# Retention and gated FFN on one core: scaled k through the crossbar, half of the masks moved from VectorE to ScalarE and GpSimd

## Chip, core and metric

The kernel runs on one core of one Trainium2 chip. The metric is the device time of one launch in microseconds (us). The engines are TensorE (PE, with its weight loads as PEld), VectorE (DVE), ScalarE (ACT), GpSimd (POOL) and SyncE (SP, which here only issues DMAs).

## The reference

Two stages follow each other. The first is a retention layer over 4 batches, 8 heads, 768 tokens and 64 features per head, with one decay per head:

```
gamma[h] = 1 - 2**(-5 - h);  scale = 1/8
state = gamma * state + outer(k[t], v[t])        # per batch and head, 64 x 64
y[t]  = scale * q[t] @ state
```

The heads of one token are then joined to a row x of 512, and a gated FFN follows: `(sigmoid(x @ w_gate) * (x @ w_val)) @ w_out`, with widths 512, 1536, 512, over 3072 rows. Inputs and output are float32; the matmuls run in bfloat16.

## The kernel before

**Tiling.** The 768 tokens are cut into 6 chunks of 128 (a chunk index is a tile t of the FFN: 4 batches x 128 tokens = 512 rows). A chunk has two pairs P of batches, so there are 12 pairs, P = 2t and 2t + 1; a pair has two batches c = 0, 1. Heads lie two by two on the 128 partitions: i = 0 the even heads, i = 1 the odd ones, p = 0 to 3 the four twos.

**Retention in a chunk.** `scores` (sc) multiplies k and q of a batch, transposed in qkT, into two PSUM banks, one for even and one for odd heads. `mask` (mk, L243) multiplies a bank by a table that holds the decay and the triangle, and writes st in bfloat16; it runs on DVE. `inter` (in) multiplies the state of the past (zbd) with q, `intra` (ia) adds v times st, `y_out` (yo) scales the sum by the row decay taby0 and writes xT, the FFN's input. `scaled` (kt, L228 and L231) makes kt, k times a decay of its token; `state` (sm) multiplies kt and v, `state_sum` (zs) adds it to the running state on DVE, `state_out` (zo, L295) copies it to zbd on ACT. The last two pairs need no kt.

**Transposing.** Pairs 0 to 3 are transposed on PE (tp, te); pairs 4 to 11 by the crossbar, a transposing DMA that SP issues (xk for k, xq for q, L219). It reads kn, the loaded k.

**Loads** are issued by POOL (L96). Pairs 6 to 11 come in three groups lk6, lq6, lv6, lk8, ..., lk10, ..., each for two pairs. Ahead of lk stands ho (`hold`, L561), a small POOL copy that reads the last element of the crossbar's output, so that the next k isn't loaded before the crossbar has read the last one.

**FFN.** From the second tile on, products of 2 x 2 blocks take 7 multiplications instead of 8: gp (gate) and vp (value) are single products into shared PSUM banks, where gc and vc (ACT copies, L430 and L409) take an intermediate value out of a bank before a later product adds onto it: product 3 of a block adds onto the bank that copy 5 has read, products 4, 6 and 7 onto the one that copy 1 has read. ga and va add on DVE, gs is the sigmoid on ACT, vf and vd multiply on POOL and DVE. dp, dc, da and ds do the same for the output projection; ds is the store. The sums that these need of weights and activations are aw, dw, wp, hg (POOL), ad, dd, xs, hs (DVE) and wc (ACT). Tile 0 and half of tile 1 use plain or half projections (gm, vm, ag, av, bg, bv) with sg, as, bs on ACT and mu, am, bm on DVE.

**Order.** Nothing is left to a scheduler. `ORDER` is a list of such steps written out, six strings, one for each tile's time; the number behind a name picks the block, + or - shift the tile by one. A step in capitals issues whole matmuls (128 columns of weights, L305), in small letters two halves of 64 columns (L309). Each engine executes its instructions in this order and waits at the first one that isn't ready. `PLACES` gives the buffer of each new tile by hand; PSUM has 7 banks for all but the state.

Of the kernel before, what the change touches and what calls it, by code (L numbers as in the profile page):

```python
# [9 lines left out]
F32 = mybir.dt.float32  # L10
# [7 lines left out]
def kernel(  # L18
# [14 lines left out]
    C = 128  # L33
# [22 lines left out]
        "ob": "01231012302130102302132031",  # L56
        "gs": "01234501234503215034203502345102354130524301453201540321453034035412031524",
        "maskd": "01",
        "ff": (
            "012345601230465102346523105426310524631205312063451623541063254165413240653016035062153621063526"  # L60
            "301263063210232534013260652605123601624302143545634210420422603216325041254246536024012416250305"
            "340153041501230163420254135426032013541354162053132620412051534"
        ),
        "qkT": "010231230123",
        "kt": "0101100101",
        "st": "012345670123456702134675120346752104637563245710",
        "xT": "010101",
        "hT": "010101",
        "scr": "010101101001101010010101010101",
# [62 lines left out]
    tok = const.tile([128, 2], F32, name="tok")  # L132
    nc.gpsimd.iota(tok, pattern=[[C, 2]], base=-C, channel_multiplier=1, allow_small_or_imprecise_dtypes=True)
# [11 lines left out]
    nc.vector.memset(lsc, math.log(scale))  # L145
    lgp = const.tile([128, NP], F32, name="lgp")
# [15 lines left out]
    tabk = const.tile([128, 2, H], F32, name="tabk")  # L162
# [13 lines left out]
    def tile_mask(i):  # L176
        nc.gpsimd.affine_select(maskd[:, i], tabk[:, 1, i:H:2].unsqueeze(2).to_broadcast([128, NP, C]),
                                pattern=[[0, NP], [1, C]], base=0, channel_multiplier=-1,
                                compare_op=ALU.is_ge, fill=0.0)

# [35 lines left out]
    def xbar(P, i):  # L216
        if P not in qkT:
            new_qkT(P)
        nc.sync.dma_start_transpose(out=qkT[P][:, i].rearrange("d c p s -> d (c p) s"),  # L219
                                    in_=(kn, qn)[i][P].rearrange("s g d -> s (g d)"))  # L220

    def scaled(P, h):
# [4 lines left out]
        if P < 4:  # L227
            nc.vector.tensor_tensor(to, x, tabk[:, 0, :].unsqueeze(1).unsqueeze(3).to_broadcast([C, 2, H, D]),  # L228
                                    op=ALU.mult)
        else:  # L230
            nc.scalar.activation(to[:, :, h, :], x[:, :, h, :], AX.Copy, scale=tabk[:, 0, h:h + 1])  # L231
# [9 lines left out]
    def mask(P, c, i):  # L241
        st[P, c, i] = place(at, [128, NP, C], BF16, tag="st", name="st")
        nc.vector.tensor_tensor(st[P, c, i], sc[P, c][i], (mask0 if P < 2 else maskd)[:, i], op=ALU.mult)  # L243
# [356 lines left out]
    y_step(1, 0, "av")  # L600
    y_step(1, 1, "av")
# [16 lines left out]
    for s in range(4):  # L618
# [61 lines left out]
        "mk": lambda t, n: mask(n // 4, n // 2 % 2, n % 2),  # L680
        "yo": lambda t, n: y_out(n // 2, n % 2),
# [115 lines left out]
```

## Time and profile before

| | |
|---|---|
| time, median of 3 runs | 217.46 us (217.25 to 217.79) |
| time of the profiled execution | 217.96 us |
| its span | 216.2 us |
| PE clock granted, mean | 0.992 |
| instructions | 7308 |
| HBM read, written | 28.31 MB, 6.29 MB |

The span runs from the first to the last instruction of the profiled execution. An engine's busy time counts its instructions' own spans; matmuls are pipelined, so that a busy PE needn't be PE at its peak. A row of a group reads: line, engine, operation, output <- inputs (partitions x elements and type), count | busy us, mean ns of one | idle us ahead of them and what ended it. A row of the chain or the timeline begins with its start and its length in us.

### The profile page before, as it was taken

What the parts mean: (1) busy time and instruction counts of PE and PEld (TensorE: products, weight loads), DVE (VectorE), ACT (ScalarE), POOL (GpSimd) and SP (SyncE); (2) the same over time, 40 slices, a digit from 0 to 9 for tenths busy, and PEclk for the clock granted to TensorE, in tenths of its full rate; (3) what the DMA queues carried; (4) which work ended last, traced back from release to release, by engine and by line L of the source; (5) the groups of instructions that cost most, each with busy time, mean ns of one, the idle gap of its engine ahead of it and who ended that gap; (6) DMA issues with size and microseconds to landing.
All of it is one profiled execution on the core that took longest, in us unless ns stands there. A gap on an engine that the chain in (4) does not pass through costs nothing.

```text
span 216.2 us, 7308 instructions
## 1 busy us (share of the span) xinstructions
PE 205.0 (95%) x3002; PEld 178.3 (82%) x3002; DVE 188.1 (87%) x406; ACT 147.8 (68%) x397; POOL 139.7 (65%) x145
## 2 busy tenths in 40 slices
PE   6678999999999999999999999989999999999993
PEld 6465555888888998898988889988999988888883
DVE  5677879899899999979999899978899999968961
ACT  6384365534993489887779798866768979577621
POOL 8976784879899946699564299756528537025400
PEclk9889999999999999999999999999999999999999
DMA  9999999999991999999992059996022000003504
GB/s 127 141 171 194 197 172 162 188 195 158 155 127 24 119 160 200 211 63 160 159 245 66 0 36 183 127 215 134 3 93 104 3 3 0 3 3 84 115 34 162
DMA packets 103922, 25.38 MB, mean 117 GB/s; under 512 B 93904, under 2 KB 101072, under 8 KB 103888
## 3 DMA queue, kind: packets, MB, share of 16 engines
q0 software_dynamic: 81104, 13.90, 83.6%
q1 hardware_dynamic: 22640, 10.88, 27.0%
q8 instruction: 23, 0.38, 0.7%
q14 instruction: 11, 0.09, 0.2%
q10 hardware_dynamic: 144, 0.13, 0.2%
HBM read 28.31 MB, written 6.29 MB: 160 GB/s over the span
## 4 chain that ended last, share of the span: by engine, by line
PE 87%; DVE 8%; issue 1%; ACT 1%; ACTq 0%; DVEq 0%
PE ff L309 39%; PE ff L305 37%; PE ff L238 3%; PE ff L258 2%; PE ff L536 2%; DVE scr L414 2%; PE ff L200 2%; PE z L280 1%; DVE hT L332 1%; DVE gs L435 1%; DVE qkT L210 1%; DVE ws L361 1%; DVE xT L273 1%; DVE kt L228 1%; ACT xT L271 1%
## 5 line engine op out<-in xcount | busy, mean ns | idle before, releaser
L420 POOL TENSOR_TENSOR hT<-gs,scr 128x512 bf16<-128x512 f32 x17 | 22.1, 1300 | 22.4 <-DVE scr L414 9.9
L430 ACT COPY gs<-ff 128x256 f32<-128x256 f32 x72 | 25.6, 377 | 11.6 <-PE ff L309 7.1
L414 DVE TENSOR_TENSOR scr<-scr,ff 128x512 f32<-128x512 f32 (+1 forms) x48 | 25.7, 550 | 4.8 <-ACT scr L409 1.5
L409 ACT COPY scr<-ff 128x256 f32<-128x256 f32 x72 | 25.2, 375 | 6.6 <-PE ff L309 3.3
L435 DVE TENSOR_TENSOR gs<-gs,ff 128x512 f32<-128x512 f32 (+1 forms) x48 | 25.8, 550 | 3.2 <-PE ff L305 2.0
L510 ACT COPY ob<-ff 128x256 f32<-128x256 f32 x48 | 17.8, 375 | 15.7 <-PE ff L305 9.2
L440 ACT ACTIVATE gs<-gs 128x512 f32<-128x512 f32 (+1 forms) x48 | 24.8, 530 | 2.8 <-DVE gs L435 2.7
L243 DVE TENSOR_TENSOR st<-ff,maskd 128x512 bf16<-128x512 f32 x40 | 25.8, 686 | 0.5 <-PE ff L238 0.4
L309 PE MATMUL ff<-xT,wg 128*64 128x256 bf16 (+1 forms) x268 | 24.0, 308 | 0.1
L309 PEld LDWEIGHTS <-wg 128*64 128x64 bf16 x356 | 19.7, 110 | 3.8 <-issue 0.2
L423 POOL TENSOR_TENSOR hT<-gs,scr 128x256 bf16<-128x256 f32 x16 | 11.9, 744 | 16.2 <-ACT gs L440 12.4
L309 PE MATMUL ff<-xT,wv 128*64 128x256 bf16 (+1 forms) x224 | 21.9, 311 | 0.0
L309 PEld LDWEIGHTS <-wv 128*64 128x64 bf16 x324 | 18.0, 110 | 4.1 <-issue 0.3
L309 PE MATMUL ff<-xs,ws 128*64 128x256 bf16 x228 | 20.5, 273 | 0.6 <-issue 0.6
L309 PEld LDWEIGHTS <-ws 128*64 128x64 bf16 x340 | 18.9, 110 | 1.4 <-issue 1.3
L305 PEld LDWEIGHTS <-wv 128*128 128x128 bf16 x178 | 17.2, 98 | 2.3
L305 PEld LDWEIGHTS <-hT 128*128 128x128 bf16 x174 | 16.8, 98 | 2.7 <-issue 0.6
L305 PEld LDWEIGHTS <-wg 128*128 128x128 bf16 x162 | 15.7, 98 | 4.1 <-issue 2.1
L231 ACT ACTIVATE kt<-kn,tabk 128x128 bf16<-128x128 bf16 x48 | 18.4, 407 | 0.1
L305 PE MATMUL ff<-xT,wv 128*128 128x256 bf16 (+1 forms) x132 | 18.1, 276 | 0.0
L305 PE MATMUL ff<-wo,hT 128*128 128x256 bf16 x132 | 17.7, 272 | 0.2 <-DVE ob L515 0.2
L305 PE MATMUL ff<-xT,wg 128*128 128x256 bf16 x110 | 15.6, 272 | 1.6 <-ACT xT L271 0.9
(119 smaller groups left out, 529.8 us busy)
## 6 DMA issues: line engine op xcount, KB each, us to landing
out_dram<-ob SPq DMA_DIRECT2D x18, 256.0 KB, 4.8
vn<-in_v_dram POOLq DMA_DIRECT2D x6, 256.0 KB, 11.9
wo<-in_moe_w_out_dram POOLq DMA_DIRECT2D x4, 384.0 KB, 13.2
kn<-in_k_dram POOLq DMA_DIRECT2D x3, 512.0 KB, 7.7
qn<-in_q_dram POOLq DMA_DIRECT2D x3, 512.0 KB, 10.0
vn<-in_v_dram POOLq DMA_DIRECT2D x3, 512.0 KB, 11.6
out_dram<-ob SPq DMA_DIRECT2D x11, 128.0 KB, 2.3
kn<-in_k_dram POOLq DMA_DIRECT2D x5, 256.0 KB, 12.1
```

The costliest lines, as they stand in the source:

```text
L231: nc.scalar.activation(to[:, :, h, :], x[:, :, h, :], AX.Copy, scale=tabk[:, 0, h:h + 1])
L243: nc.vector.tensor_tensor(st[P, c, i], sc[P, c][i], (mask0 if P < 2 else maskd)[:, i], op=ALU.mult)
L305: nc.tensor.matmul(o, left, right, skip_group_check=True, **kw)
L309: nc.tensor.matmul(o[half], left[:, half], right, skip_group_check=True, **kw)
L409: nc.scalar.copy(vals[t, g][:, {1: 0, 5: 2, 3: 1}[n]], m[False][:, 256:] if n == 1 else m[True][:, :256])
L414: nc.vector.tensor_tensor(o, o, x, op=ALU.add)
L420: eng.tensor_tensor(h[:, 2 * g], s, vals[t, g][:, 0:2].rearrange("p two n -> p (two n)"), op=ALU.mult)
L423: eng.tensor_tensor(h[:, 2 * g + 1, 256:], s[:, 256:], vals[t, g][:, 2], op=ALU.mult)
L430: nc.scalar.copy(o, pairs[t, g, 0][x][:, :256] if x else pairs[t, g, 0][x][:, 256:])
L435: nc.vector.tensor_tensor(o, o, pairs[t, g, 0][False][:, cols], op=ALU.add)
L440: nc.scalar.activation(o, x, AX.Sigmoid)
L510: nc.scalar.copy(o, fast[t, i][x][:, :256] if x else fast[t, i][x][:, 256:])
```

## The change

The decays are rearranged so that one scaling of k serves both the scores and the state. The token table loses its offset: kt is now k times gamma^(-s) with s the place in the chunk, and the row decay taby0 has gamma^(C + t) instead of gamma^t (C = 128).

For pairs 4 to 9 the crossbar reads kt instead of kn. Their scores then carry the token's decay already, and what is left of the mask is a constant per head, gamma^(-C), and the triangle. The even heads' masks of these pairs stay DVE multiplications, with a new table maskc, built by one POOL select (mt0). The odd heads' masks (12 of them) are split into two steps: mc, four ACT copies of 128 columns from PSUM with the constant as scale, and ms, one POOL select in place that cuts the triangle. The crossbar of these pairs now waits for the eight scalings of its pair.

The scaling of pairs 2 and 3 goes from one DVE instruction to eight on ACT. The outputs of pair 1's two batches are written by DVE and ACT, one each, where before both engines wrote half of each. ORDER and PLACES are new throughout; among much else 9 of the hs sums go to POOL (hg), 5 of the POOL sums aw to DVE (ad), and 4 of the products vf to DVE (vd).

```diff
-    tok = const.tile([128, 2], F32, name="tok")
-    nc.gpsimd.iota(tok, pattern=[[C, 2]], base=-C, channel_multiplier=1, allow_small_or_imprecise_dtypes=True)
+    tok = const.tile([128, 3], F32, name="tok")
+    nc.gpsimd.iota(tok[:, :2], pattern=[[C, 2]], base=0, channel_multiplier=1, allow_small_or_imprecise_dtypes=True)
...
+    nc.vector.memset(tok[:, 2:], float(C))
...
+    def chunk_mask(i):
+        if not maskc:
+            maskc[0] = place(at, [128, 2, NP, C], F32, tag="maskd", name="maskc")
+        nc.gpsimd.affine_select(maskc[0][:, i], tabk[:, 2, i:H:2].unsqueeze(2).to_broadcast([128, NP, C]),
+                                pattern=[[0, NP], [1, C]], base=0, channel_multiplier=-1,
+                                compare_op=ALU.is_ge, fill=0.0)
...
-                                    in_=(kn, qn)[i][P].rearrange("s g d -> s (g d)"))
+                                    in_=(qn if i else kt if P < NPAIR - 2 else kn)[P].rearrange("s g d -> s (g d)"))
...
-        if P < 4:
+        if P < 2:
             nc.vector.tensor_tensor(to, x, tabk[:, 0, :].unsqueeze(1).unsqueeze(3).to_broadcast([C, 2, H, D]),
...
-        nc.vector.tensor_tensor(st[P, c, i], sc[P, c][i], (mask0 if P < 2 else maskd)[:, i], op=ALU.mult)
+        nc.vector.tensor_tensor(st[P, c, i], sc[P, c][i], (mask0 if P < 2 else maskd if P < XBAR or P > NPAIR - 3 else maskc[0])[:, i],
+                                op=ALU.mult)
+
+    def mask_copy(P, c, i):
+        st[P, c, i] = place(at, [128, NP, C], BF16, tag="st", name="st")
+        for p in range(NP):
+            nc.scalar.activation(st[P, c, i][:, p], sc[P, c][i][:, p], AX.Copy, scale=math.exp(-C * lg[2 * p + i]))
+
+    def mask_cut(P, c, i):
+        nc.gpsimd.affine_select(st[P, c, i], st[P, c, i], pattern=[[0, NP], [1, C]], base=0, channel_multiplier=-1,
+                                compare_op=ALU.is_ge, fill=0.0)
...
-    y_step(1, 0, "av")
-    y_step(1, 1, "av")
+    y_step(1, 0, "v")
+    y_step(1, 1, "a")
```

The parts of the new order of which the prediction speaks, first from the scores of pairs 4 and 5 to tile 1's products, then around lk8:

```diff
+ ... sm5 sc9 mk18 sc8 mk16 dw22 zs5 mc19 mc17 ms17 BG8 DP03- wc5 DP16- dd17 ms19 zo4 BV4 IN8 dd2 sc11 in9 ia9
+ bs8 ho5 in10 ia8 sm4 mc23 lk6 sc10 mc21 DP02- bm4 DP01- dc01- wp11 mk22 IN11 zo11 dc03- wc4 yo9 BV8 da16-
+ mk20 kt49+ kt52+ ad2 yo8 dw18 zs4 kt53+ kt59+ bm8 GP21+ gp22+ ms23 gc21+ kt57+ ad6 kt61+ ia11 kt58+ yo11
+ dp06-- da06-- av8- ms21- ia10- yo10- zo10- xs0 dp17-- da17-- dp07-- gp05 gc05 gp25 gc25 kt48 DP14-- dc14--
+ ds14-- GP15 am8- kt50 hs4- xs2 da07-- GP23 ...
+ ... VP15 kt62 sm7 VP07 xk6- ... xq6- ... xk7- ... ds16-- ... GP36 xq7- ... vf16 ho7 ... sc12 ... sc15 mc31 lk8
+ ... gp55 lq8 lv8 gc55 ia12 kt71 VP51 vc51 GP46 GP53 gc53 zs7 kt65 mk26 GP51 da16- DP17- vc41 gc51 ... GP56 ...
```

More of the change, by code (lines that the diff above doesn't have):

```diff
@@ L55 @@
         "v": "010101",
-        "ob": "01231012302130102302132031",
-        "gs": "01234501234503215034203502345102354130524301453201540321453034035412031524",
-        "maskd": "01",
+        "ob": "01231030321023032103121032",
+        "gs": "01234501235435012453205431501423051402530104521325402153201421401235042135",
+        "maskd": "010",
         "ff": (
-            "012345601230465102346523105426310524631205312063451623541063254165413240653016035062153621063526"
-            "301263063210232534013260652605123601624302143545634210420422603216325041254246536024012416250305"
-            "340153041501230163420254135426032013541354162053132620412051534"
-        ),
-        "qkT": "010231230123",
-        "kt": "0101100101",
-        "st": "012345670123456702134675120346752104637563245710",
+            "012345601230465102346523105426314021635160412036412041362413062541520145634163041203621042310423"
+            "142324064216524131305416521504250423623164120210524163131321205234123465254054315614316216345040"
+            "534605364632304210651613402605240512631261204356462412032122543"
+        ),
+        "qkT": "012301230123",
+        "kt": "0120102010",
+        "st": "012345670123456703216745021345670265741326507413",
         "xT": "010101",
         "hT": "010101",
-        "scr": "010101101001101010010101010101",
+        "scr": "010110011001101010100110010101",
     }
@@ L161 @@
         nc.vector.memset(z, 0.0)
-    tabk = const.tile([128, 2, H], F32, name="tabk")
+    tabk = const.tile([128, 3, H], F32, name="tabk")
     tabz = const.tile([128, NP], F32, name="tabz")
@@ L177, in tile_mask @@
         nc.gpsimd.affine_select(maskd[:, i], tabk[:, 1, i:H:2].unsqueeze(2).to_broadcast([128, NP, C]),
+                                pattern=[[0, NP], [1, C]], base=0, channel_multiplier=-1,
+                                compare_op=ALU.is_ge, fill=0.0)
+    maskc = {}
+    def chunk_mask(i):
+        if not maskc:
+            maskc[0] = place(at, [128, 2, NP, C], F32, tag="maskd", name="maskc")
+        nc.gpsimd.affine_select(maskc[0][:, i], tabk[:, 2, i:H:2].unsqueeze(2).to_broadcast([128, NP, C]),
                                 pattern=[[0, NP], [1, C]], base=0, channel_multiplier=-1,
@@ L680 @@
         "mk": lambda t, n: mask(n // 4, n // 2 % 2, n % 2),
+        "mc": lambda t, n: mask_copy(n // 4, n // 2 % 2, n % 2),
+        "ms": lambda t, n: mask_cut(n // 4, n // 2 % 2, n % 2),
+        "mt": lambda t, n: chunk_mask(n),
         "yo": lambda t, n: y_out(n // 2, n % 2),
```

148 rows, old and new, of the table ORDER are left out of this document.

## The prediction, made before the changed kernel was run

> **What bounds the kernel now.** I read the page's engine totals and its chain of waits first, then the stretches (busy time by window), then the chain in order of time.
>
> ```profile
> PE 205.0 (95%) x3002; PEld 178.3 (82%) x3002; DVE 188.1 (87%) x406; ACT 147.8 (68%) x397; POOL 139.7 (65%) x145
> ```
> ```profile
> PE 87%; DVE 8%; issue 1%; ACT 1%; ACTq 0%; DVEq 0%
> ```
> ```profile
> 0.00:18.70 18.70, 12.61 (x156) 10.64 (x156) 11.85 (x32) 11.96 (x32) 15.22 (x23) 0.91 1.70 152
> 32.00:36.00 4.00, 3.67 (x58) 2.28 (x56) 3.93 (x10) 3.59 (x5) 2.88 (x4) 1.00 2.16 167
> 108.00:112.00 4.00, 3.85 (x77) 3.38 (x72) 3.90 (x9) 2.67 (x8) 3.25 (x3) 1.00 1.42 211
> 140.00:152.00 12.00, 11.02 (x206) 10.39 (x204) 9.84 (x27) 8.26 (x25) 7.64 (x8) 1.00 1.05 159
> 176.00:204.00 28.00, 27.94 (x256) 24.74 (x254) 24.72 (x56) 20.83 (x63) 11.15 (x11) 1.00 0.14 32
> 204.00:212.90 8.90, 8.56 (x76) 7.10 (x74) 5.55 (x14) 2.49 (x7) 0.00 (x0) 1.00 0.31 98
> ```
> ```profile
> 64.35 0.55 PE ff L238 x16
> 69.63 0.37 PE z L280 x16
> 132.16 0.22 PE ff L258 x8
> 140.54 0.64 issue
> 147.85 0.34 issue
> 176.70 24.47 PE ff L305 x222
> ```
>
> The first number of a stretch after its length is PE's busy time. PE is idle for 6.1 us before 18.7 us, where the operands first arrive. From there to 212.9 us its idle time is 0.33 + 0.15 + 0.98 + 0.06 + 0.34 = 1.9 us in these five stretches, and none in the others. Of that, 0.98 us (140 to 152 us) is "issue", which no engine ended; 0.9 us is the most that a relieved VectorE (DVE) can give back. PE is granted its full clock (1.00) after the start, and 222 matmuls of 256 columns take 24.47 us, 0.110 us each. The steps of the order hold the same count of matmuls after the change as before (168 gate products, 168 value products, 84 down products, 24 half projections, 22 whole ones, the same scores; some only change between the form of two halves and the whole form). So PE's own work doesn't move: the change can win 0.9 us in the middle and something at the two ends, and it loses every wait that the new order brings to PE.
>
> **The change, part by part.** Engine work first, from the groups of instructions by line and shape.
>
> ```profile
> L243 DVE TENSOR_TENSOR st<-ff,maskd 128x512 bf16<-128x512 f32 x40 | 25.8, 686 | 0.5 <-PE ff L238 0.4
> L228 DVE TENSOR_TENSOR kt<-kn,tabk 128x1024 bf16<-128x1024 bf16 x4 | 4.9, 1218 | 0.0
> L231 ACT ACTIVATE kt<-kn,tabk 128x128 bf16<-128x128 bf16 x48 | 18.4, 407 | 0.1
> L177 POOL TENSOR_SCALAR_AFFINE_SELECT maskd<-tabk 128x512 f32<-128x512 f32 x2 | 1.2, 644 | 0.0
> L295 ACT CAST zbd<-za 64x512 bf16<-64x512 f32 x20 | 12.4, 618 | 4.5 <-DVE za L287 2.6 <-DVE za L290 0.9 <-PE ff L305 0.8
> ```
> ```profile
> 77.32 0.62 ACT L430 COPY gs<-ff 128x256 f32<-128x256 f32 x2
> 110.89 0.69 ACT L231 ACTIVATE kt<-kn,tabk 128x128 bf16<-128x128 bf16 x2
> ```
>
> DVE loses 12 masks (25.8/40 = 0.65 us each, 7.7 us) and two scalings of k (1.22 us each, 2.4 us): 10.1 us of 188. ScalarE (ACT) gains 16 scalings (18.4/48 = 0.38 us each, 6.1 us) and 48 copies of 128 columns. The trace has no such copy. Two copies of 256 columns take 0.62 us, so the second adds 0.25; half of it, 0.13, is the low end. Two scalings of 128 columns take 0.69, so the second adds 0.30: the high end. I take 0.20, between them, because the copy has the shape of the one and the fixed scale of the other. One mask's four copies are then 0.8 us (0.5 to 1.2), and ACT has 148 + 6 + 10 = 164 us of 216. GpSimd (POOL) gains 13 selects, priced at the 0.64 us of L177, 8.4 us. Neither engine is full on average, so what matters is who waits for whom.
>
> ```profile
> L474 DVE TENSOR_TENSOR hs<-hT,hs x13: 411/424/1379, 56.5 to 206.7; 128x512 bf16<-128x512 bf16 x13
> L474 DVE TENSOR_TENSOR hs<-hs,hT x12: 414/420/1375, 28.2 to 204.6; 128x512 bf16<-128x512 bf16 x12
> ```
>
> The DVE gain is worth at most the 0.9 us above. Against it, some DVE sums with two SBUF operands already take 1.38 us where the median is 0.42, and the selects put more POOL reads beside them; I take 0.7 us of gain (0 to 0.9). The Trainium skill ("SBUF — State Buffer", section "Who interferes with whom") says that a VectorE instruction with two SBUF inputs and a GpSimd instruction that reads SBUF exclude each other, and the second blocks fully. By that rule, which the 1.38 us agree with, the select could cost DVE what its masks saved, and the 0.7 would be 0.
>
> **Scaling ahead of the crossbar.** A scaling now stands between k's load and k's crossbar, and the order puts scalings into ACT's queue soon after the load's issue. An engine works in order, so everything behind such a scaling waits for the load.
>
> ```profile
> kn<-in_k_dram POOLq DMA_DIRECT2D x3, 512.0 KB, 7.7
> vn<-in_v_dram POOLq DMA_DIRECT2D x3, 512.0 KB, 11.6
> qkT<-kn SPq DMA_TRANSPOSE x8, 8.0
> qkT<-qn SPq DMA_TRANSPOSE x8, 6.0
> ```
> ```profile
> 68.62 0.18 POOL L561 COPY kept<-qkT 128x2 bf16<-128x2 bf16 x1
> 68.75 1.72 POOL L96 DMA_DIRECT2D kn<-in_k_dram  x1
> ```
> ```profile
> 77.01 0.40 ACT L231 ACTIVATE kt<-kn,tabk 128x128 bf16<-128x128 bf16 x1
> ```
>
> Before, the load of pairs 6 and 7 (lk6) was issued at 68.75 us, landed 7.7 us later (76.5), and the first scaling that needs it ran at 77.0: nothing waited. After, POOL must make two masks (ms17, ms19) before ho5 and lk6, and they wait for ACT's copies, which wait for the scores. Counted from the start of step sc8: two copy steps 1.6 + 0.1, two selects 1.3, ho5 0.15, so lk6 goes out at 3.15 and lands at 10.85. ACT comes to kt49 at 8.4: PE is through IN11 at 6.9, and zo11, dc03 and wc4 follow (1.5). There it waits; behind kt49 lie kt52, kt53, kt59 (with kt49 4 x 0.30 = 1.2), gc21 (0.27), kt57, kt61, kt58 (0.9), zo10 (0.62), gc05 (0.27), gc25 (0.38): gc25 is done at 14.5. PE's step GP23 adds onto the bank that gc25 reads and can't start before. PE's work from sc8 to GP23, by the new order: 3 scores at 0.28, 4 half projections at 8 x 0.11 = 0.88, 8 down products at 0.66, 8 inter or intra steps at 0.22, one state step 0.37, 5 products at 0.22: 0.84 + 3.52 + 5.28 + 1.76 + 0.37 + 1.10 = 12.9. PE waits **1.6 us**. With 0.5 or 1.2 us for a mask's copies it is 1.0 or 2.4.
>
> The Trainium skill ("DMA: Bandwidth & Descriptors", section "Anatomy of one DMA — SWDGE (gpsimd) path") fits such a load as 2.0 us plus its bytes over 436 GB/s, an estimate of 3.2 us for 512 KB. By that k would land at 6.4, before ACT comes to it, and the wait would be 0; the row of 7.7 us disagrees, and the row decides.
>
> The same again for pairs 8 and 9: xq7 (6.0 us to land) releases ho7 and lk8 (7.7 us), and the order puts kt71 close behind. From xq7's place in the order, 0.2 + 6.0 + 7.7 = 13.9, then kt71, vc51, gc53, kt65, vc41, gc51 (1.8 us) before PE's GP56: 15.7, where PE has 13.1 us of work between (GP36 at its place to GP56, summed in the same way). That is 2.6 us if SP issues xq7 at its place; SP may run ahead by up to the 3.5 us since VP15 (kt62, the last scaling that xk7 needs, follows it), and then it is nothing. I take **0.9** (0 to 2.6). The first crossbars of pairs 4 and 5 have room: their scores come some 10 us after the scalings. The load of v for pair 7 (lv6) stands behind a POOL sum that waits for DVE (hg5 for hs4), about 9 us before sm7 uses it: nothing at the 7.7 us of k, 2.4 us at the 11.6 of v, where other loads were in flight; I take 0, and the 2.4 goes to the range.
>
> **Both ends.**
>
> ```profile
> L148 DVE MEMSET lgp<- 64x1 f32 x8 | 0.5, 59 | 0.3
> ```
> ```profile
> 16.72 0.38 ACT xT L268
> 17.12 0.77 DVE xT L269 x2
> 17.93 0.81 PE ff L305 x6
> ```
> ```profile
> 212.36 0.38 ACT ob L510
> 212.76 0.37 ACTq L531
> 213.23 0.37 ACT ob L510
> ```
>
> The start gains one memset ahead of the identity (about 0.1 us) and splits pair 1's output by half instead of within each half: DVE waited until 17.12 for ACT and PE until 17.93; one instruction on each engine should save 0.15 us or, if the two writes to one tile are put in sequence, cost 0.3. I take 0 for the start (-0.3 to 0.4). At the end the order puts dc04 ahead of dc14, so ACT's store issue (0.37 us and its gaps) no longer stands before the last copy: **-0.4** (-0.5 to 0).
>
> Sum on the profiled execution (217.96 us, 1.8 us over its span of 216.2): 217.96 + 1.6 + 0.9 - 0.7 - 0.4 = 219.4. The median of the runs is 217.46, 0.5 below that execution, so I forecast **218.9 us**.
>
> **Rivals.** (1) Faster: ACT's holds are hidden, because k lands sooner (less traffic beside it) or PE arrives later at GP23 and GP56 for other reasons. Both waits go, and the time is 217.46 - 0.7 - 0.4 = 216.4; with the start's best, 216.0, and if the "issue" idle went too, 215.1. It decides at about 6 us for lk6: from there the hold is hidden. For it: PE has waits that I don't foresee, which shorten these. Against it: all three k loads of this size have a median of 7.7. Chance 0.29.
> (2) No change: one wait is half hidden, the gains cancel the rest: 217.46 - 1.1 + 1.2 = 217.6. Chance 0.13.
> (3) Worse: the copies take 0.30 us each, v is late for sm7 and xq7 leaves at its place: 217.46 + 2.4 + 2.4 + 2.6 - 1.1 = 223.8; with two of the three 221.4. ACT, then, is the bound between 70 and 110 us. Chance 0.13.
> (4) The relief doesn't come, since the selects hold DVE: 219.6, within my forecast's case, which has 0.45 with it.
>
> The measurement tells about 0.3% (0.65 us) from no change. Slower is the forecast's case and (3), 0.58; within 0.3% is (2), 0.13; faster is (1), 0.29. The range leaves out the best of (1) and the worst of (3): 215.4 to 222.0.
>
> **What would show it.** In the changed profile: ACT idle before L231 with a DMA of kn as what ended it, some 3 us near 74 us and again near 104; PE idle 1 to 2 us near 80 us, ended by ACT's copy; POOL's masks of 0.64 us; DVE near 178 us busy; the last copy not behind a store issue. Wrong it is if ACT shows no such wait, if lk6 lands in under 6 us, or if PE's idle time between 18.7 us and the end is under 1.9 us.

## The result, and the profile after

The changed kernel takes 224.44 us (median of 4 runs, 222.85 to 232.78), the kernel before 217.62 us beside it (217.25 to 217.79). The ratio is 1.029, with a 95% interval of 1.023 to 1.035. The forecast was 218.9 us, in a range of 215.4 to 222.0: slower was right, the size was not. The ratios here and below leave out executions more than 1.5% above the fastest of their kernel.

The profiled execution of the changed kernel is the longest of its four (232.78 us), so I also read the profile of a second, unaltered submission, called the repeat here (223.82 us, span 222.0). First the busy times and the chain of the changed kernel's page, then of the repeat's:

```profile
PE 208.8 (90%) x3050; PEld 178.8 (77%) x3050; DVE 189.4 (82%) x392; ACT 158.2 (68%) x460; POOL 151.5 (66%) x158
PE 64%; DVE 14%; DMA 7%; POOL 5%; ACT 4%; issue 4%; DVEq 0%; POOLq 0%; ACTq 0%
```
```profile
PE 206.3 (93%) x3050; PEld 177.5 (80%) x3050; DVE 185.7 (84%) x392; ACT 158.4 (71%) x460; POOL 151.3 (68%) x158
PE 71%; DVE 21%; ACT 4%; issue 2%; POOL 1%; DVEq 0%; POOLq 0%
```

PE's share of the chain fell from 87% to 64 and 71%; DVE, DMA and POOL stand there in its place. And DVE, with 189.4 and 185.7 us, is about as busy as before (188.1), although it lost some 10 us of work. The stretches of 44 to 84 us, first of the repeat and then of the kernel before, say where (after the length come the busy times of PE, PEld, DVE, ACT and POOL):

```profile
44.00:62.00 18.00, 14.98 (x256) 13.99 (x256) 16.27 (x26) 11.01 (x29) 14.49 (x14) 1.00 1.94 160
62.00:84.00 22.00, 21.14 (x333) 18.38 (x330) 20.61 (x43) 16.94 (x53) 17.36 (x21) 1.00 0.88 73
```
```profile
44.00:62.00 18.00, 18.00 (x219) 15.71 (x217) 16.93 (x31) 12.05 (x28) 16.46 (x16) 1.00 1.96 166
62.00:84.00 22.00, 22.00 (x383) 20.20 (x381) 21.47 (x46) 14.28 (x39) 18.07 (x19) 1.00 1.50 114
```

PE loses 3.0 us between 44 and 62 us, a place of which the prediction has no term, and 0.9 us between 62 and 84, the place of its first wait. In the timeline, the repeat's PE waits there twice, for a mask and for a product of DVE; the changed kernel's first profile has one wait of 9.1 us:

```profile
48.93 1.03 PE L326 MATMUL ff<-xT,wv 128*128 128x256 bf16 x8 [1.45 <-DVE st L254]
58.74 1.06 PE L330 MATMUL ff<-xT,wv 128*64 128x256 bf16 x16 [1.58 <-DVE hT L370]
```
```profile
57.85 1.86 PE L326 MATMUL ff<-xT,wv 128*128 128x256 bf16 x8 [9.08 <-DVE st L254]
```

In the first profile eight matmuls took 1.86 us after that wait, in the repeat 1.03. The page's row of the granted clock, in slices of 5.8 us, says why:

```profile
PEclk9999999995599999999999999999999999999998
```

It is 0.5 for two slices, 52 to 63.6 us, that is from within the wait to some 5 us behind it; at half the clock those 5 us held some 2 us less work (an estimate). What held DVE stands in its own timeline and in POOL's, in the repeat:

```profile
45.91 2.37 DVE L495 TENSOR_TENSOR hs<-hT,hs 128x512 bf16<-128x512 bf16 x1
48.20 1.28 DVE L254 TENSOR_TENSOR st<-ff,maskd 128x512 bf16<-128x512 f32 x2
53.79 0.28 DVE L382 TENSOR_TENSOR ws<-wv 128x256 bf16<-128x256 bf16 x1
53.99 4.10 DVE L382 TENSOR_TENSOR ws<-wg,ws 128x256 bf16<-128x256 bf16 x1
58.01 0.68 DVE L370 TENSOR_TENSOR hT<-gs,ff 128x512 bf16<-128x512 f32 x1
```
```profile
45.66 1.14 POOL L96 DMA_DIRECT2D vn<-in_v_dram  x1 [0.58 <-DMA wo<-in_moe_w_out_dram]
46.82 1.17 POOL L477 TENSOR_TENSOR scr<-wo 128x512 f32<-128x512 bf16 x1
47.94 0.83 POOL L187 TENSOR_SCALAR_AFFINE_SELECT maskc<-tabk 128x512 f32<-128x512 f32 x1
48.74 1.15 POOL L477 TENSOR_TENSOR scr<-scr,wo 128x512 f32<-128x512 f32 x1
...
55.67 1.15 POOL L477 TENSOR_TENSOR wt<-wo,scr 128x512 bf16<-128x512 bf16 x1
56.79 1.14 POOL L477 TENSOR_TENSOR scr<-wo 128x512 f32<-128x512 bf16 x1
60.80 1.16 POOL L477 TENSOR_TENSOR scr<-scr,wo 128x512 f32<-128x512 f32 x1 [2.87 <-ACT wt L481]
```

From 46.82 us, right behind the issue of a load, to 57.9 us POOL runs ten sums and a select without a pause, seven of them the weight sums wp of L477, each reading two SBUF operands. A DVE sum with two SBUF operands that takes 0.29 us alone took 4.10 us and ended at 58.09, just behind POOL's row. The sum at 45.91 (0.42 us alone) began during the issue of the load and ended at 48.28, behind the first weight sum. The issue can hold such a sum too: in the kernel before one of 0.29 us took 0.72 at 29.72, beside nothing else. The masks of L254, with one operand in PSUM, ran beside the same POOL sums in 0.64 us each.

The first profile has four long sums in a row there, of 2.05, 2.97, 2.86 and 3.11 us, each ending shortly behind the end of a POOL instruction, but the last three not behind the first that ended: the one below passed the ends at 48.88 and 49.99 and ended at 51.28, behind the third, at 51.10.

```profile
48.31 2.97 DVE L382 TENSOR_TENSOR ws<-wv 128x256 bf16<-128x256 bf16 x1
```

The kernel before has the same weight sums, and most of DVE's instructions beside them have a PSUM operand. But nine DVE sums with two SBUF operands run there too, between 46.9 and 66 us, and none took over 1.38 us: the seven that were held each ended shortly behind the POOL instruction that was running. Three of them, and POOL's instruction beside the last two:

```profile
51.20 1.24 DVE L361 TENSOR_TENSOR ws<-wv,ws 128x256 bf16<-128x256 bf16 x1
56.51 1.38 DVE L474 TENSOR_TENSOR hs<-hT,hs 128x512 bf16<-128x512 bf16 x1
60.99 1.24 DVE L361 TENSOR_TENSOR ws<-ws,wg 128x256 bf16<-128x256 bf16 x1
```
```profile
56.27 1.34 POOL L456 TENSOR_TENSOR wt<-wo,scr 128x512 bf16<-128x512 bf16 x1
60.75 1.34 POOL L474 TENSOR_TENSOR hT<-hT 128x512 bf16<-128x512 bf16 x1
```

So the new order doesn't bring more such sums beside POOL's. What differs in this stretch is that DVE got its turn at the end of one POOL instruction in the kernel before, and in the changed kernel mostly behind several. Why, no run here shows.

### The profile page after: what moved, and what is told of

Its sections match the earlier page's. It is cut to its first block, busy times and chain, and to the rows that moved or that the text cites. A ratio compares the mean times of both kernels' runs of the same rounds, so it can differ in the third digit from the quotient of the medians.

```text
span 231.1 us, 7467 instructions
## 1 busy us (share of the span) xinstructions
PE 208.8 (90%) x3050; PEld 178.8 (77%) x3050; DVE 189.4 (82%) x392; ACT 158.2 (68%) x460; POOL 151.5 (66%) x158
## 4 chain that ended last, share of the span: by engine, by line
PE 64%; DVE 14%; DMA 7%; POOL 5%; ACT 4%; issue 4%; DVEq 0%; POOLq 0%; ACTq 0%
PE ff L330 33%; PE ff L326 27%; DMA vn<-in_v_dram 4%; DVE hs L495 4%; DMA kn<-in_k_dram 4%; DVE scr L435 3%; DVE xT L294 2%; PE ff L249 2%; DVE ws L382 1%; PE ff L279 1%; DVE gs L456 1%; PE z L301 1%; ACT kt L242 1%; ACT gs L461 1%; ACT zbd L316 1%
## 5 line engine op out<-in xcount | busy, mean ns | idle before, releaser
L330 PE MATMUL ff<-xT,wv 128*64 128x256 bf16 (+1 forms) x300 | 27.0, 304 | 0.0
L330 PEld LDWEIGHTS <-wv 128*64 128x64 bf16 x400 | 21.4, 110 | 4.4 <-issue 0.7
L242 ACT ACTIVATE kt<-kn,tabk 128x128 bf16<-128x128 bf16 x64 | 22.3, 395 | 3.0 <-DMA kn<-in_k_dram 3.0
L326 PE MATMUL ff<-xT,wv 128*128 128x256 bf16 x94 | 15.0, 285 | 9.1 <-DVE st L254 9.1
L326 PEld LDWEIGHTS <-wv 128*128 128x128 bf16 x140 | 13.6, 100 | 11.7 <-issue 9.6
L495 POOL TENSOR_TENSOR hs<-hs,hT 128x512 bf16<-128x512 bf16 x9 | 10.7, 1192 | 17.2 <-DVE hs L495 10.0
L330 PE MATMUL ff<-xs,ws 128*64 128x256 bf16 x200 | 18.1, 274 | 0.1
L326 PE MATMUL ff<-xT,wg 128*128 128x256 bf16 (+1 forms) x98 | 16.2, 293 | 1.7 <-ACT xT L292 1.7
L366 ACT ACTIVATE gs<-ff 128x512 f32<-128x512 f32 x12 | 6.8, 593 | 14.1 <-PE ff L330 13.1
L326 PEld LDWEIGHTS <-ws 128*128 128x128 bf16 x136 | 13.0, 98 | 3.8 <-issue 1.8
```

Of the source, the lines that this page charges most:

```text
L326: nc.tensor.matmul(o, left, right, skip_group_check=True, **kw)
L330: nc.tensor.matmul(o[half], left[:, half], right, skip_group_check=True, **kw)
L366: nc.scalar.activation(gated[t, n1, half], us[t, n1, half, 0], AX.Sigmoid)
L495: eng.tensor_tensor(o, x, z, op=op)
```

## The experiments

The theory behind the first runs (**shared port**): a DVE sum with two SBUF operands doesn't get on while POOL reads SBUF in instruction after instruction; the mask queued behind it comes late, and PE waits. Its rivals: the **hold** of the prediction (ACT waits for the load lk6) and the **order** itself (masks that now need three engines, a DVE without slack).

**The repeat.** No edit.

> The changed kernel unaltered, for a second profile of it. Port theory (VectorE's sums of two SBUF operands are held by GpSimd's instructions, and the masks of pair 3 queue behind them): 223 to 225 us; the four sums hs5, ad20, ad21 and hs11, 0.28 to 0.42 us each where nothing runs beside them, take 8 us or more together again, and PE stands 5 us or more before AV2. Hold theory (ScalarE waits at a scaling for the load of k): PE loses 1 to 2.4 us before GP23, and the rest of the 6 us lies in similar holds.

Measured: 223.77 us (223.08 to 231.79), ratio 1.0285 (1.0259 to 1.0311). The place is the same in both profiles, the size is not (9.1 us, and 1.45 + 1.58 us; 5 us or more before AV2 were expected).

**Sums moved later.** In the order of tile 1, five DVE sums that stood ahead of the late mask:

```diff
- ... hs9- hs2- sc7 kt28 AG4 kt24 AG0 hs5- as4 AG2 hs7- ad20 ad21 hs11- mk15 AV4 ...
+ ... hs9- hs2- sc7 kt28 AG4 kt24 AG0 as4 AG2 mk15 AV4 ... yo6 hs5- hs7- hs11- ... ad14 ad20 ad21 ...
```

> The changed kernel with five VectorE sums moved behind what PE waits for: hs5, hs7, hs11 behind yo6, and ad20, ad21 behind ad14. Port theory: the wait before AV2 goes, the time falls by 5 to 7 us to 217 to 219; the moved sums may still be slow, but nothing urgent is behind them. Hold theory: unchanged, 223 to 225, with 1 to 2.4 us lost before GP23 in either case.

Measured: 228.45 us (227.01 to 230.08), ratio 1.049 (1.042 to 1.056). The wait before AV2 went, and the time rose by 5 us, against the expectation: a moved sum met the same row of POOL sums later.

```profile
51.93 5.72 DVE L495 TENSOR_TENSOR hs<-hs,hT 128x512 bf16<-128x512 bf16 x1
```

PE then waited 4.2 us for the product behind it, and its granted clock was 0.50 from 58.6 to 65 us. The wait moved with the sums, as the theory has it, but the new place was no better: POOL's row went on to 57.4 us.

**Scalings moved later.** Seven scalings of k, which stand behind the load lk6 in ACT's queue, go behind gc25:

```diff
- ... da16- mk20 kt49+ kt52+ ad2 yo8 dw18 zs4 kt53+ kt59+ bm8 GP21+ gp22+ ms23 gc21+ kt57+ ad6 kt61+ ia11 kt58+ yo11
+ ... da16- mk20 ad2 yo8 dw18 zs4 bm8 GP21+ gp22+ ms23 gc21+ ad6 ia11 yo11
+ ... gc25 kt49 kt52 kt53 kt59 kt57 kt61 kt58 kt48 ...
```

> The changed kernel with the seven scalings kt49, 52, 53, 59, 57, 61, 58 moved behind gc25 in ScalarE's queue, so that gc21 and gc25 don't wait for the load of k. Hold theory: PE's wait before GP23 (1.2 us in the profile after) goes, 222 to 223 us. Port theory: this wait goes too, but the long one before AV2 stays, so no more than 1.2 us are won.

Measured: 230.01 us (226.87 to 233.85), ratio 1.044 (1.041 to 1.047). PE no longer waits before GP23, but in this profile a sum of DVE took 5.74 us beside POOL's row (PE: 3.2 us), and PE waited 1.1 us for an ACT copy behind the moved scalings and 1.8 us for v before sm7. With the contention on, its size changes from run to run and hides effects of 1 us.

**Masks back on DVE.** Nine of the twelve odd masks are DVE multiplications again, and their selects fall away. POOL builds the table maskc for the odd heads too (mt), one select more in its row at 48 us (AT_MS is empty, so mask_place is never used):

```diff
+    AT_MC, AT_MS = (17, 19, 23, 25, 29, 31, 33, 35, 37), ()
...
-        "mc": lambda t, n: mask_copy(n // 4, n // 2 % 2, n % 2),
-        "ms": lambda t, n: mask_cut(n // 4, n // 2 % 2, n % 2),
-        "mt": lambda t, n: chunk_mask(n),
+        "mc": lambda t, n: (mask if n in AT_MC else mask_place if n in AT_MS else mask_copy)(n // 4, n // 2 % 2, n % 2),
+        "ms": lambda t, n: None if n in AT_MC else (mask_now if n in AT_MS else mask_cut)(n // 4, n // 2 % 2, n % 2),
+        "mt": lambda t, n: [chunk_mask(0), chunk_mask(1)],
```

> The changed kernel with 9 of the 12 odd masks (all but those of steps 21, 27 and 39) back on VectorE as one multiplication each, in the place of their ScalarE copies; k is still scaled ahead of the crossbar. If moving the masks costs the time: 219 to 221 us. If it is paid by VectorE: 9 x 0.65 us more on VectorE, of which PE sees 0 to 3 us: 224 to 227. Port theory: the wait before AV2 is untouched (these masks come later), 223 to 226.

Measured: 229.11 us (228.12 to 239.76), ratio 1.053 (1.048 to 1.058), some 5 us over the repeat and above every expectation. PE waits 2.7 us before AV2, so part of this can be the added select in POOL's row. In this order the masks' move off DVE helps; taking it back alone doesn't undo the loss.

**POOL's weight sums taken away**, in the changed kernel and in the kernel before: each becomes two memsets of its destination, together as long as the sum, and the products that use the sums get zeros.

```diff
-        nc.gpsimd.tensor_tensor(o, x, z, op=op)
+        for _ in range(2):
+            nc.gpsimd.memset(o, 0.0)
```

> The changed kernel, with each of the twelve weight sums on POOL (wp, L477) replaced by two POOL memsets of the same destination, which read nothing from SBUF. The down products of the Strassen-like blocks then use zeros in place of these sums; all counts of instructions on PE, DVE and ACT stay. Shared-port theory (DVE sums with two SBUF operands starve while POOL reads SBUF in instruction after instruction): the DVE sums between 44 and 60 us last 0.28 to 0.45 us each, none over 1.5; PE's waits before AV2 and av6 (1.6 and 1.7 us in the repeat of the changed kernel, 9.2 in the first profile) vanish, the wait of 0.9 us before GP23 stays, and the time is 219.5 to 221.0. Rival, the order itself brings the waits (masks on ACT and POOL, late loads): the DVE sums get short but PE's waits stay, 223 to 224.5.

> The kernel before, with each of its twelve weight sums on POOL replaced by two POOL memsets of the same destination; the down products of the blocks use zeros for them. Shared-port theory: the DVE sums that last up to 1.38 us fall to 0.45 us, but PE waited for none of them, so the time is 216.8 to 217.6. Rival, memsets speed up any order by what they spare (power, memory traffic): it falls by as much as the changed kernel's does, 213.5 to 215.

Measured: the changed kernel 221.14 us (220.92 to 222.31), ratio 1.018 (1.014 to 1.023), just above what was expected; the kernel before 217.78 us (217.26 to 219.0), ratio 1.0015 (0.9995 to 1.0035). DVE's timeline of the first:

```profile
45.69 0.29 DVE L382 TENSOR_TENSOR ws<-ws,wv 128x256 bf16<-128x256 bf16 x1
45.90 0.42 DVE L496 TENSOR_TENSOR hs<-hT,hs 128x512 bf16<-128x512 bf16 x1
46.23 1.28 DVE L254 TENSOR_TENSOR st<-ff,maskd 128x512 bf16<-128x512 f32 x2
52.37 0.29 DVE L382 TENSOR_TENSOR ws<-wg,ws 128x256 bf16<-128x256 bf16 x1
```
```profile
44.00:62.00 18.00, 18.00 (x312) 17.13 (x311) 14.81 (x34) 14.29 (x38) 16.46 (x28) 1.00 1.95 164
62.00:84.00 22.00, 20.25 (x316) 17.35 (x314) 17.67 (x40) 15.98 (x53) 15.10 (x20) 1.00 1.05 87
```

The sums that took 2.37 and 4.10 us take 0.42 and 0.29; PE has no idle time between 44 and 62 us, with POOL busier there (16.46 us) than in the repeat (14.49). The two memsets last 1.1 us, as the sum did. So it is POOL's reading and not its being busy. This is worth some 2.5 us of time (223.77 to 221.14, and 1.0285 to 1.018 by the ratios), and nothing in the kernel before. What is left between 62 and 84 us is the hold: PE's wait before GP23 is 1.74 us, twice the expected 0.9.

```profile
80.55 0.38 PE L326 MATMUL ff<-xT,ws 128*128 128x256 bf16 x2 [1.74 <-ACT gs L451]
77.04 1.27 ACT L242 ACTIVATE kt<-kn,tabk 128x128 bf16<-128x128 bf16 x4 [2.71 <-DMA kn<-in_k_dram]
68.26 1.72 POOL L96 DMA_DIRECT2D kn<-in_k_dram  x1
```

**Scalings later, without the weight sums.** Both edits together.

> As the kernel with memsets in place of POOL's weight sums, and seven scalings of k (kt49, 52, 53, 59, 57, 61, 58) behind gc25 in ACT's queue, so that nothing that PE needs at GP23 stands behind the load lk6. Hold theory beside the shared port: the wait before GP23 (0.9 us) goes and nothing takes its place, 0.7 to 1.2 us under the kernel with memsets alone, so 218.5 to 220.0. Rival: the moved scalings make later steps late (sm7 or gp11), as they did with the sums left on POOL, and the time is the same as or above the kernel with memsets, 220 to 222.

Measured: 221.65 us (220.99 to 224.6), ratio 1.018 (1.014 to 1.022), the same as without the move. The wait before GP23 is gone and PE waits for a copy behind the block of scalings instead (80.81 us, 1.09 us, and 0.29 us after it). The rival was right.

**The wait for the load taken away, and the end as before.** The scalings of pairs 6 and 7 read k of pairs 4 and 5, in the same places of ACT's queue; DP04 and its store come last again.

```diff
-        x = kn[P].rearrange("s (c h) d -> s c h d", c=2)
+        x = kn[P - 2 if P in (6, 7) else P].rearrange("s (c h) d -> s c h d", c=2)
```
```diff
- DP13 hg10 dc11 DP16 hg6 dp07 dc13 da16 DP17 da07 ds07 DP04 dc04 ds16 da17 DP14 ds17 dc14 ds14 ds04
+ DP13 hg10 dc11 DP16 hg6 dc13 da16 ds16 DP17 dp07 da17 ds17 da07 ds07 DP14 dc14 ds14 DP04 dc04 ds04
```

> The changed kernel with memsets in place of POOL's weight sums (as before: those products use zeros), and two things more. The scalings of pairs 6 and 7 read k of pairs 4 and 5, which has long landed, in the same places of ACT's queue, so nothing in ACT's queue waits for lk6 (scores and states of pairs 6 and 7 use the wrong k). And the last 19 steps of the order end as the kernel before does: DP16, ds16, ds17, then DP14 with its store, then DP04 with its store. Hold theory: the wait of 1.9 us before GP23 vanishes and nothing takes its place up to sm7; tail theory: from the start of PE's last step to the end of the span it is 4.1 us as before, not 4.8; together 221.1 - 1.9 - 0.8 = 218.4 (217.8 to 219.2). Rival to the first: ACT is full there and GP23, gp11 or sm7 still wait 1 us or more, 219.5 to 221. Rival to the second: the tail stays at 4.8, 219.0 to 219.6.

Measured: 220.42 us (219.96 to 222.91), ratio 1.015 (1.006 to 1.023): 0.7 us less where 2.7 was expected of the two edits together, and not clear of the noise.

```profile
80.55 1.72 POOL L96 DMA_DIRECT2D vn<-in_v_dram  x1
89.26 0.44 PE L301 MATMUL z<-vn,kt 128*64 128x64 bf16 x16 [1.00 <-DMA vn<-in_v_dram]
212.16 0.81 PE L326 MATMUL ff<-wo,hT 128*128 128x256 bf16 x6 [0.83 <-DVE ob L537]
215.36 0.37 ACT L532 COPY ob<-ff 128x256 f32<-128x256 f32 x1 [0.44 <-PE ff L326]
```

The wait before GP23 is gone, and PE, now earlier, meets the next late load: v of pair 7, issued at 80.55, landed 8.7 us later, and sm7 waited 1.0 us for it. At the end, 3.1 us pass from the start of the last copy (215.36) to the end of the span (218.5), as in the kernel before (213.23 to 216.2, 3.0 us); with the changed kernel's own end it is 3.9 (the repeat, 218.06 to 222.0). But in this order of the end PE waits 0.8 us for DVE between DP16 and DP17, which gives that back.

**Masks back on DVE, without the weight sums.** Both edits together.

> Memsets in place of POOL's weight sums (zeros as before), and nine of the twelve odd masks back on DVE as multiplications. It asks what the moved masks are worth without the contention: with POOL's sums on, putting them back cost some 5 us. Theory that DVE has no slack in this order's middle: they cost 2 to 5 us again, 223 to 226. Theory that the 5 us came of masks queued behind starving sums: 0 to 1 us, 221 to 222.

Measured: 225.55 us (224.67 to 226.66), ratio 1.036 (1.030 to 1.043), 4.4 us over the same kernel with the masks on ACT and POOL. PE waits 2.4 us for a product of DVE within a batch's scores (at 105.4 us). The loss doesn't need POOL's weight sums, then. It fits an order that has spent the 10 us that DVE was relieved of and has no room to take them back, which is argued from this one wait.

**The weight sums on DVE**, first eleven of them, then six other POOL sums of the stretch too, then this with the end as before and the seven scalings moved singly behind seven copies. All three compute the reference in full.

```diff
-        nc.gpsimd.tensor_tensor(o, x, z, op=op)
+        (nc.gpsimd if g == 2 and i == 3 else nc.vector).tensor_tensor(o, x, z, op=op)
```

> The changed kernel with the full computation, eleven of the twelve weight sums moved from POOL to DVE (wp0 to wp2 behind mk12, wp3 and wp4 behind yo6, wp5 behind am2, wp6 behind bm6, wp7 and wp8 behind zs2, wp9 behind bm10, wp10 behind bm0; wc2 behind wc3). Shared-port theory: with POOL's chain gone no DVE sum lasts over 1.5 us between 44 and 60 us; DVE has 11 sums more there, 0.4 to 0.7 us each (5 to 8 us in some 18 us that are about two thirds full), which may make masks late by 1 to 2 us: 219 to 222, with a smaller spread than the changed kernel. Rival, DVE is simply too full there: it is late by more than the contention cost, 224 to 228.

> The full computation. As the kernel with eleven weight sums on DVE, and the six other POOL sums of that stretch (aw13, aw11, aw0, dw20, dw14, hg10) on DVE too, so that POOL runs no sum between 45 and 62 us. Shared-port theory: the six DVE sums ahead of mask mk15, which took 5.9 us beside POOL's sums with the weight sums moved, take 2.1 again, the wait of 3.3 us before AV2 falls under 0.5, and the time is 219.5 to 221.5. Rival, DVE is too full with the 17 sums more (some 9 us): a wait of over 2 us before AV2 or a later step, 223 to 226.

> The full computation, as the kernel with all sums of the stretch on DVE, with the order's end as before (DP04 and its store last) and the seven scalings of k behind lk6 moved singly behind gc25, gc03, gc01, gc13, vc21, vc25 and vc23. Port, hold and tail theories together: 219.5 to 221.5 less 0.8 (tail) less 1.0 to 1.9 (hold) gives 217.0 to 219.5. Rival: the copies of values that now stand behind single scalings come late at gp11 to VP26 as they did behind the block of seven, and the gain of the spread is 0: 218.7 to 220.7.

Measured: 226.82 us (223.04 to 228.24); 225.66 (221.61 to 228.09), ratio 1.025 (1.011 to 1.039); 224.35 (221.81 to 225.37), ratio 1.027 (1.016 to 1.037). None is clearly better than the changed kernel. In the first, POOL's remaining sums still stand in one row at 47 to 51 us, and a DVE sum among them takes 1.86 us; PE waits 3.2 us before AV2. In the second no sum ahead of mask mk15 takes over 0.89 us, and the wait before AV2 is 0.5 us, near what was expected; the time is not. With 17 sums more on DVE, PE's waits of 0.5 to 1.3 us are spread over six places from 51 to 153 us, four of them for DVE. In the third, PE's longest wait behind the start is 1.9 us of "issue" near 152 us, whose cause stays open.

**A gap between POOL's sums.** A POOL memset of 2 elements (0.1 us) or of 256 (0.3 us) per partition behind each weight sum, the full computation:

```diff
         nc.gpsimd.tensor_tensor(o, x, z, op=op)
+        nc.gpsimd.memset(gap, 0.0)
```

> The changed kernel, full computation, with a POOL memset of 2 elements per partition (about 0.1 us, reads nothing) behind each of POOL's twelve weight sums. Theory that DVE needs a gap in the row of POOL's sums: each DVE sum gets in at the next memset, so none between 44 and 60 us lasts over 1.6 us, PE's waits before AV2 and av6 fall to under 0.7 together, and the time is 220.8 to 222.3, little above the 221.1 with memsets in place of the sums. Rival, a gap of 0.1 us is too short to be let in (the next sum is already issued): DVE sums of 2 to 5 us remain and the time is 223 to 226. Rival, the wait is for one POOL instruction in any case and the long sums had another cause: nothing changes, 223 to 225.

> The same with a longer memset behind each weight sum, 256 float32 elements per partition, about 0.27 us, 3.2 us more POOL work in all. Gap theory: DVE sums under 1.6 us whatever the short gap does, time 220.8 to 222.8 (POOL's later sums and selects come up to 3 us later, which may cost 0 to 0.5). Rival (no effect of gaps): 223 to 226.

Measured: 230.1 us (226.65 to 236.16) and 228.48 us (227.2 to 236.83; ratio 1.048, 1.044 to 1.052). Both are worse. DVE and POOL with the short gap:

```profile
52.64 6.12 DVE L382 TENSOR_TENSOR ws<-wv 128x256 bf16<-128x256 bf16 x1
```
```profile
52.28 1.15 POOL L478 TENSOR_TENSOR wt<-wo 128x512 bf16<-128x512 bf16 x1
53.37 0.09 POOL L479 MEMSET gap<- 128x2 bf16 x1
53.43 1.15 POOL L478 TENSOR_TENSOR wt<-wo 128x512 bf16<-128x512 bf16 x1
...
57.48 1.14 POOL L478 TENSOR_TENSOR scr<-wo 128x512 f32<-128x512 bf16 x1
```

One DVE sum waited through six POOL sums and the memsets between them and ended at 58.76, behind the last sum (58.62). With the long gap one sum still took 4.34 us, three others 1.25 to 1.37, each ending behind one POOL sum. A short instruction that reads nothing doesn't let DVE in reliably; what does, stays open.

**One operand read.** Each weight sum becomes a POOL copy of its first operand.

```diff
-        nc.gpsimd.tensor_tensor(o, x, z, op=op)
+        nc.gpsimd.tensor_copy(o, x)
```

> The changed kernel with each of POOL's weight sums replaced by a POOL copy of its first operand into the same destination (one operand read in place of two; those products of the blocks then use unsummed weights). Theory that any POOL reading holds DVE's sums: they still take 1 to 5 us beside the copies, time 222 to 225. Theory that it takes two operands: DVE sums of 0.28 to 0.45 beside the copies, time 220.5 to 221.7 as with memsets.

Measured: 221.13 us (220.51 to 221.46), ratio 1.016 (1.013 to 1.019), as with memsets.

```profile
46.29 1.27 DVE L495 TENSOR_TENSOR hs<-hT,hs 128x512 bf16<-128x512 bf16 x1
```
```profile
46.65 0.62 POOL L477 CAST scr<-wo 128x512 f32<-128x512 bf16 x1
47.22 0.83 POOL L187 TENSOR_SCALAR_AFFINE_SELECT maskc<-tabk 128x512 f32<-128x512 f32 x1
```

Both theories are half right. A DVE sum beside a reading cast took 1.27 us, three times its own time, and ended behind the cast, so one operand read holds it too. But the copies take 0.6 us where the sums took 1.15, POOL's row is shorter (to 53.2 us), and no other DVE sum stood in its midst; how much is owed to the second operand, this run can't say.

## Why the prediction was wrong in size

**The step that failed: the DVE term.** The prediction had -0.7 us there and, where "the selects hold DVE", 0. It saw the sums of 1.38 us and cited the rule that bears on them, but asked only what the added selects would do, and let the loss go no further than the gain. The selects cost little: beside selects DVE sums of 0.28 us took 0.57 to 0.74 in the first profile and the repeat (in the run with the long gap one took 2.09 us, beside a sum, two selects and the issue of a load). What the prediction put at nothing is POOL's old weight sums: in the new order they hold DVE's sums over several POOL instructions, up to 4.10 us in the repeat, where the order before had at most 1.38. That cost PE 3.0 us in the repeat and 9.1 in the first profile; without the weight sums the time falls by some 2.5 us and its spread to 1.4. So 1.38 us was no worst case, but the longest that the old order happened to show. That the weight sums do it is shown by the memsets; why DVE missed its turn in the new order and not in the old one stays open.

The Trainium skill ("SBUF — State Buffer", section "Who interferes with whom") also states that POOL instructions which only write don't contend and that a DVE instruction with at most one SBUF input, outside the modes that use both of its ports, doesn't: the memsets (0.42 us where it was 2.37) and the masks (0.64 us beside the weight sums) agree. It speaks of a block for the length of the instruction that came first; the 6.12 us beside POOL sums of 1.15 us are more than that.

**The hold at GP23** was right: 1.6 us (1.0 to 2.4) was forecast, and 1.74 measured in PE's row with POOL's weight sums away. Both sides of the difference came later than summed, the load with 8.8 us for 7.7 and PE with 13.7 us from sc8 to GP23 for 12.9; that they nearly cancel is luck. In the repeat PE lost 0.8 us there. It came 3.5 us later than without the weight sums, but that is not what shortened the wait, as rival (1) would have it ("PE has waits that I don't foresee, which shorten these"): lk6 too went out 3.4 us later (71.64 for 68.26), and its load took 7.9 us instead of 8.8. That the term would be worth little if removed was not foreseen: v for sm7 is late right behind it, the case that the range held at 2.4 us, and sm7 then waited 1.0 us.

**The hold at GP56** (0.9, 0 to 2.6) didn't come: in the first profile, the repeat and the run with memsets ACT doesn't wait for lk8's k, and PE has no wait there. In the repeat lk8 went out at 100.47 us, its k landed at 107.33, and the scaling that needs it ran at 107.78.

**The masks' costs** were right: four copies 0.8 us, a select 0.64. In the repeat, a group by line, and a row of the timeline:

```profile
L263 POOL TENSOR_SCALAR_AFFINE_SELECT st<-st 128x512 bf16<-128x512 bf16 x12 | 7.4, 640 | 2.4 <-ACT st L260 2.4
```
```profile
72.69 0.79 ACT L260 ACTIVATE st<-ff 128x128 bf16<-128x128 f32 x4 [1.02 <-PE ff L249]
```

So was "DVE near 178 us", once the weight sums don't hold it: 179.2 us without them. The rest of the 189.4 and 185.7 is waiting that counts as busy.

**The tail** was mis-signed: -0.4 forecast, +0.9 measured. The last copy no longer stands behind a store's issue, as said, but the last two stores are now issued at the same time, close behind another, and what follows the copy grew from 3.0 to 3.9 us:

```profile
218.06 0.37 ACT L531 COPY ob<-ff 128x256 f32<-128x256 f32 x1 [0.30 <-PE ff L326]
218.47 0.40 ACTq L552 DMA_DIRECT2D out_dram<-ob  x1
218.50 0.38 SPq L552 DMA_DIRECT2D out_dram<-ob  x1
```

**The start** was right in the repeat (0); in the first profile PE waited 1.3 us more, for a load of v.

Sum for the repeat, from span to span (216.2 to 222.0, 5.8 us): 3.0 beside the weight sums, 0.9 between 62 and 84 us, 0.9 in the tail. The other 1.0 us is no wait: PE's idle time outside these three is the same in sum, and its busy time is 206.3 us against 205.0. Where that comes from is not shown; the busy time of the kernel before reads 205.9 us itself in the run without its weight sums. No version that was run beats the kernel before.

## What to carry to other kernels

When an order is rewritten, ask of each DVE instruction with two SBUF operands which row of POOL's reading instructions it now falls beside. Price it with a range, from one POOL instruction (1.38 us in the old order) to the rest of the row (6.12 us in one run), not by the longest such instruction that the old order shows. When a wait is removed, look for the load or the copy that is late next before counting the gain: taking away the hold of 1.7 us, and the longer tail with it, gave 0.7 us, within the noise, and the next load was 1.0 us late.

## What was not expected of the hardware

A DVE sum of 0.29 us beside back-to-back POOL sums of 1.15 us was held for up to 6.12 us, through three memsets that read nothing, while in the kernel before such sums got their turn behind one POOL instruction. DVE's busy time includes this, so that an engine relieved of 10 us of work looked as busy as before. And in an idle time of 9.1 us PE's granted clock fell to half, and stayed there for some 5 us behind it. Behind waits of 3.2 and 2.4 us it fell too: with the scalings moved later it was 0.50 from 58.6 to 62.0 us, and 16 matmuls took 1.92 us; with the masks back on DVE and without the weight sums it was 0.51 from 106.5 to 109.9 us. Behind the repeat's waits of 1.45 and 1.58 us it stayed at 1.00, and 16 took 1.06. So a wait of PE can cost more than its own length.
